# Attention backward for one query: dK of the previous pair ahead of the K blocks in the first turns

## The chip, the core and the metric

The kernel runs on one core of a Trainium2 chip. The core has TensorE (PE in the profile: matmuls, transposes, with PEld its weight loads), VectorE (DVE), ScalarE (ACT), GpSimdE (POOL) and SyncE (SP), each with its own instruction queue, worked in order; 16 DMA engines move data between the memory (HBM) and the on-chip memory (SBUF). TensorE writes to PSUM, the accumulator memory of eight banks. The metric is device time in microseconds (us) of one execution, lower is better.

## The reference

One query row per head attends to 8192 keys, for 32 heads of width 128, all in bfloat16; output and all three gradients are wanted.

```
scores = einsum('bhqd,bhkd->bhqk', q, k) * 128 ** -0.5     # 1 query, 8192 keys, 32 heads
attn   = softmax(scores)
out    = einsum('bhqk,bhkd->bhqd', attn, v)                # out_0
# vjp with grad_out (dO):
dP = dO . V^T        dS = attn * (dP - sum(attn * dP)) * 128 ** -0.5
dq = dS K  (out_1)   dK = dS^T q  (out_2)   dV = attn^T dO  (out_3)
```

K and V are 67.1 MB each and are read once; dK and dV are as large and are written once: 268.4 MB in all. dK and dV are outer products of a column of 8192 weights with a row of 128.

## The kernel before, in words

Heads go in pairs: pair j is heads 2j and 2j+1, 16 pairs, one turn of the main loop (L308) each, and a seventeenth turn that only finishes the last pair. K and V of a pair are one tile each, 128 partitions by 128 rows of 128 elements (4096 KB), `Kt[j]` and `Vt[j]`; three K tiles and two V tiles are held (`K_BUFS`, `V_BUFS`). dK and dV are written in place over `Kt[j]` and `Vt[j]` by VectorE and stored from there. All large transfers are issued from SP's queue in program order (`load_k`, `load_v`, `outer`). A load of K(j+2) needs the store of dK(j-1) to have landed (three buffers), a load of V(j+1) that of dV(j-1) (two buffers).

The steps of a pair, with the names that the change touches:

- K scores: `k_blocks` (L164) transposes an eighth of K in 32x32 blocks on VectorE into one of three `XK_sb` buffers; `k_scores` (L169) multiplies it by the query, four matmuls into `s_ps`. `blocks(n)` does both for the next n of the eight blocks, and only the second for a block that has been transposed already.
- Softmax: `s_back` turns the scores back (VectorE), maximum, `top`, a TensorE transpose into the shared bank `m_ps`, `nbias`, exponential (ScalarE), sum by a matmul, `rinv`, then `p_rep` and `window("p")` on ScalarE, and `p_s` on VectorE.
- V scores (dP): `v_transposes` (L186) turns four 128x128 squares of V on TensorE into one of three `T_ps` banks, `v_copy` (L196) copies the bank on ScalarE into `XV_sb`, and after eight such groups `v_scores` (L200) does 16 matmuls for half of the keys.
- `contract` (L234): 32 matmuls in 8 rounds of 4, of p with V (`acc_p`, which gives out) or dS with K (`acc_ds`, which gives dq). `gather_copy` copies the accumulator to SBUF, `gather` (L248) sums it by eight small matmuls into `m_ps` and copies two columns to `o_all` or `dq_all`.
- `v_back`, `pd_sum`, `ds_of`: dP is turned back, multiplied by the exponentials and summed, and dS is formed, its window on ScalarE.
- `outer` (L257): one eighth of dV or dK as one multiply on VectorE over the tile; it has to wait for the round of `contract` that reads this eighth. After the eighth one the store is issued. The last dK is stored in four quarters and the last dV in two halves (`PARTS`).
- `result` (L298): transposes `o_all` or `dq_all` and stores it from the one buffer `fin_sb`.

In each turn j the work of pair j (K scores, softmax, then V transposes, contraction with p and dV together, L409 to L418) is interleaved with what is left of pair j-1 (dP, dS, contraction with dS, dK). There are two forms, chosen by `ends` (L310). In the overlapped form (turns 2 to 15) the contraction with dS stands between the K blocks, and the eight multiplies of dK are spread: two before the softmax, two in its waits (L373, L389), four behind it. In the serial form (turns 0, 1 and 16) the contraction and the whole of dK stand after the second K block, the other K blocks follow (L342 to L357), and V transposes fill the waits of the softmax on TensorE. The order on each engine is as the program writes it (`manual_schedule`): there is no planner.

In the last turn the order is: `pd_sum`, `ds_of`, gather of out, its store, contraction with dS, eight multiplies of dK with four stores, and ahead of the fourth the gather of dq and its store (L346 to L348).

Of the kernel before, what the change touches and what calls it, by code (L numbers as in the profile page):

```python
# [14 lines left out]

XK_BUFS = 3
PARTS = {("dk", -1): 4, ("dv", -1): 2}
CH = 16
TB = 4
# [7 lines left out]
def kernel(  # L27
# [168 lines left out]
    def v_copy(j, c):  # L196
        b = c % (NX // TB)
        nc.scalar.copy(XV[j][:, b * TB:(b + 1) * TB, :], st[j].pop(("T", c))[:])  # L198
# [107 lines left out]

    DQ = NG // 4
    for j in range(HP + 1):  # L308
        p_ = j - 1
        ends = j in (0, 1, HP)  # L310
        x = st.setdefault(j, {})
        todo = list(range(NU)) if j < HP else []

        def blocks(n):
            for u in todo[:n]:
                if (j, u) not in XK:
                    k_blocks(j, u)
                k_scores(j, u)
            del todo[:n]

        if j == 0:
# [3 lines left out]
            q_window(0)  # L325
        blocks(1)
        if j > 0:
            v_back(p_)
            pd_sum(p_)
        blocks(1 if ends else 2)  # L330
        if j == 0:
            first = psT.tile([P, 512], F32, tag="T", name="first")
            rows_bc(0, first[:, 256:512])
            do_columns()
            do_window(0)
        if j > 0:
            ds_of(p_)
            gather(p_, "p", st[p_]["m"])
            if j == HP:
                result(o_all, out_0)  # L340
        if ends and j > 0:
            contract(p_, "ds", 0, NG)  # L342
            gather_copy("ds")
            for r in range(NU):
                outer(p_, "dk", r)
                if j == HP and r == NU - 3:  # L346
                    gather(p_, "ds", st[p_]["m"])
                    result(dq_all, out_1)  # L348
            if j + 1 < HP:
                load_v(j + 1)  # L350
        if j == HP:
            break
        for i in range(4):
# [14 lines left out]
        nc.tensor.transpose(x["m"][:, 128:256], top[:].to_broadcast([P, P]), ident_f[:])  # L368
        if ends:
            v_transposes(j, 0)  # L370
            v_transposes(j, 1)
        else:
            outer(p_, "dk", 2)  # L373
        nbias = small.tile([P, 1], F32, tag="nbias")
        for t in range(2):
# [6 lines left out]
                         skip_group_check=True)  # L382
        if ends:
            v_copy(j, 0)
            v_copy(j, 1)
            v_transposes(j, 2)
            v_transposes(j, 3)
        else:
            outer(p_, "dk", 3)  # L389
# [5 lines left out]
        x["p_s"] = small.tile([P, NT], F32, tag="p_s", name="p_s")  # L395
        nc.vector.tensor_scalar(x["p_s"][:], e[:], rinv[:], scale, op0=ALU.mult, op1=ALU.mult)
        if not ends:
            gather(p_, "ds", x["m"])
        if j + 1 < HP:
            rows_bc(j + 1, x["m"][:, 256:512])  # L400
            q_window(j + 1)
        if not ends:
            for r in range(4, NU):
                outer(p_, "dk", r)
            if j + 1 < HP:
                load_v(j + 1)
        elif j > 0:
            gather(p_, "ds", x["m"])
        for r in range(NU):  # L409
            for c in (2 * r, 2 * r + 1):  # L410
                if not (ends and c < 4):
                    v_transposes(j, c)
                if not (ends and c < 2):
                    v_copy(j, c)
            contract(j, "p", 4 * r, 4 * r + 4)
            if r % 4 == 3:
                v_scores(j, r // 4)
            outer(j, "dv", r)  # L418
# [3 lines left out]
        if 0 < j and j + 2 < HP:  # L422
            load_k(j + 2)

    order.__exit__(None, None, None)

# [29 lines left out]
```

## Time and profile before

| | |
|---|---|
| time, median of 3 runs | 645.21 us (642.86 to 646.59) |
| the profiled execution | 644.92 us, span 643.1 us |
| DVE busy | 518.9 us (81%) |
| PE busy | 501.6 us (78%), mean granted clock 0.832 |
| ACT busy | 223.2 us (35%) |
| SP's transfers | 268.46 MB in 97.8% of the 16 engines' span |
| HBM over the span | 417 GB/s |

The span runs from the first instruction to the last; the time has 1.8 us more around it. Busy time is of instructions, not of useful work: PE at a granted clock of 0.5 is busy for longer with the same matmuls. The slices of the page are 40 equal ones, 16.1 us each. A DMA issue is a short instruction on SP's queue (SPq), and what it moves comes later, behind all that was issued before. `Kt` and `Vt` are both loaded and stored: `Kt<-in_k_dram` is a load, `out_dram<-Kt` the store of dK.

### The profile page before, as it was taken

Reading aid. Unit: us, or ns where it says so; the run is one execution under the profiler, and the core shown is the slowest. Engines: PE = TensorE matmul, PEld = TensorE weight load, DVE = VectorE, ACT = ScalarE, POOL = GpSimd, SP = SyncE. Lnnn points to the kernel's source line nnn. Section 1 sums busy time; section 2 is a strip of 40 time slices with the busy share of each in tenths; the row PEclk is TensorE's granted clock in tenths of the full one; section 3 lists DMA queues with packets and bytes.
Section 4 is the critical chain, followed back from the end, with each engine's and each line's share of the span. In section 5 each row is a group of like instructions: output and inputs, shape, how many; then the busy total and the mean of one; then the engine's idle time right before and its main releaser. Section 6 shows DMA issues by size and latency. Waiting matters only on the chain.

```text
span 643.1 us, 8528 instructions
## 1 busy us (share of the span) xinstructions
PE 501.6 (78%) x3480; PEld 284.9 (44%) x3480; DVE 518.9 (81%) x654; ACT 223.2 (35%) x508; POOL 3.2 (0%) x10
## 2 busy tenths in 40 slices
PE   4885887878798787879777798787879778798780
PEld 1441534445363544536354363444526345363550
DVE  5678598887979888797887977889797887978873
ACT  2430524325151432515143160442515235151440
POOL 1000000000000000000000000000000000000000
PEclk9976897879978687997878886788897779878785
DMA  8999988999999999999999999999999999999996
GB/s 365 442 431 421 423 336 360 374 438 423 427 435 429 426 429 438 419 429 439 429 428 432 439 425 427 438 431 431 429 438 428 430 436 429 431 427 427 403 416 271
DMA packets 11318, 269.01 MB, mean 418 GB/s; under 512 B 1424, under 2 KB 1424, under 8 KB 1424
## 3 DMA queue, kind: packets, MB, share of 16 engines
q1 hardware_dynamic: 11184, 268.46, 97.8%
q8 instruction: 27, 0.44, 0.3%
q14 instruction: 11, 0.09, 0.0%
q10 hardware_dynamic: 96, 0.02, 0.0%
HBM read 134.23 MB, written 134.23 MB: 417 GB/s over the span
## 4 chain that ended last, share of the span: by engine, by line
PE 43%; DMA 32%; DVE 18%; ACT 4%; issue 2%; ACTq 0%; SPq 0%; DVEq 0%
DMA Kt<-in_k_dram 19%; PE s_ps L176 15%; PE T_ps L193 13%; DMA out_dram<-Kt 11%; DVE XK_sb L166 5%; DVE Kt L261 5%; PE m_ps L253 4%; PE acc_p L240 4%; PE acc_ds L240 4%; ACT XV_sb L198 2%; PE dp_ps L210 2%; DMA out_dram<-fin_sb 2%; DVE Vt L261 2%; DVE sT L183 1%; DVE dpT L221 1%
## 5 line engine op out<-in xcount | busy, mean ns | idle before, releaser
L261 DVE TENSOR_TENSOR Vt<-p_rep,qd 128x2048 bf16<-128x2048 bf16 x128 | 156.4, 1225 | 63.4 <-PE acc_p L240 52.7
L176 PE MATMUL s_ps<-XK_sb,q_win 128*128 128x512 bf16 x512 | 154.3, 437 | 46.4 <-DVE XK_sb L166 41.2
L193 PE MATMUL T_ps<-ident_f,Vt 128*128 128x128 f32 x1024 | 170.9, 321 | 0.0
L198 ACT COPY XV_sb<-T_ps 128x512 f32<-128x512 f32 x256 | 140.5, 588 | 87.2 <-PE T_ps L193 87.1
L166 DVE STREAM_TRANSPOSE XK_sb<-Kt 128x1024 f32<-128x1024 f32 x128 | 151.3, 1221 | 19.3 <-DMA Kt<-in_k_dram 11.1
L261 DVE TENSOR_TENSOR Kt<-ds_rep,qd 128x2048 bf16<-128x2048 bf16 x128 | 149.7, 1215 | 5.0 <-PE acc_ds L240 4.5
L193 PEld LDWEIGHTS T_ps<-ident_f,Vt 128*128 128x128 f32 x1024 | 136.3, 165 | 37.8 <-issue 22.1
L176 PEld LDWEIGHTS <-q_win 128*128 128x128 bf16 x512 | 51.6, 111 | 132.0 <-issue 102.5
L240 PE MATMUL acc_p<-Vt,win_p 128*32 128x512 bf16 x512 | 57.1, 439 | 0.8 <-ACT win_p L232 0.8
L210 PE MATMUL dp_ps<-XV_sb,do_win 128*32 128x512 bf16 x512 | 34.8, 385 | 12.4 <-ACT XV_sb L198 12.3
L240 PE MATMUL acc_ds<-Kt,win_ds 128*32 128x512 bf16 x512 | 41.6, 414 | 0.0
L246 ACT COPY S_ds<-acc_ds 128x512 f32<-128x512 f32 x16 | 9.4, 585 | 92.9 <-PE acc_ds L240 92.9
L232 ACT COPY win_ds<-ds 64x128 bf16<-64x128 bf16 x32 | 9.5, 296 | 79.3 <-DVE ds L291 79.1
L380 ACT ACTIVATE e<-sT,nbias 128x128 f32<-128x128 f32 x16 | 8.3, 516 | 69.9 <-DVE nbias L376 69.9
L253 PE MATMUL m_ps<-lane,S_ds 128*128 128x2 f32 x128 | 26.3, 327 | 6.1 <-DVE rinv L391 4.3
L253 PEld LDWEIGHTS m_ps<-lane,S_ds 128*128 128x128 f32 x128 | 24.9, 290 | 8.0 <-DVE rinv L391 5.5
L381 PE MATMUL m_ps<-rs,ones_f 128*128 128x1 f32 x32 | 8.2, 324 | 25.2 <-ACT e L380 25.2
L210 PEld LDWEIGHTS <-do_win 128*32 128x32 bf16 x512 | 14.3, 94 | 28.7 <-issue 21.9
L240 PEld LDWEIGHTS <-win_p 128*32 128x32 bf16 x512 | 13.2, 94 | 26.6 <-issue 26.3
L368 PE MATMUL m_ps<-ident_f,top 128*128 128x128 f32 x16 | 4.7, 296 | 23.7 <-DVE top L366 23.7
L183 DVE STREAM_TRANSPOSE sT<-s_ps 128x512 f32<-128x512 f32 x16 | 11.5, 717 | 14.2 <-PE s_ps L176 14.2
L240 PEld LDWEIGHTS <-win_ds 128*32 128x32 bf16 x512 | 9.6, 100 | 27.2 <-issue 27.2
(59 smaller groups left out, 207.0 us busy)
## 6 DMA issues: line engine op xcount, KB each, us to landing
Kt<-in_k_dram SPq DMA_DIRECT2D x15, 4096.0 KB, 29.2
out_dram<-Vt SPq DMA_DIRECT2D x15, 4096.0 KB, 28.0
out_dram<-Kt SPq DMA_DIRECT2D x15, 4096.0 KB, 22.3
Vt<-in_v_dram SPq DMA_DIRECT2D x14, 4096.0 KB, 28.9
Vt<-in_v_dram SPq DMA_DIRECT2D x8, 1024.0 KB, 19.7
Kt<-in_k_dram SPq DMA_DIRECT2D x4, 1024.0 KB, 8.1
out_dram<-Vt SPq DMA_DIRECT2D x2, 2048.0 KB, 15.1
out_dram<-Kt SPq DMA_DIRECT2D x4, 1024.0 KB, 9.7
```

Of the source, the lines that this page charges most:

```text
L166: nc.vector.transpose(XK[j, u][:].rearrange("p g w i -> p (g w i)"), slots(Kt[j], u, NU).rearrange("p g d -> p (g d)").bitcast(F32))
L176: nc.tensor.matmul(st[j]["s"][:], lhsT=q_win[:, c, at:at + P], rhs=cols[:, c // 2, c % 2], start=(u == 0 and c == 0), stop=(u == NU - 1 an ...
L183: nc.vector.transpose(sT[:].rearrange("p g r -> p (g r)"), x["s"][:])
L193: nc.tensor.transpose(T_ps[:, i, :], words[:, m * P:(m + 1) * P], ident_f[:])
L198: nc.scalar.copy(XV[j][:, b * TB:(b + 1) * TB, :], st[j].pop(("T", c))[:])
L210: nc.tensor.matmul(out[b * QD:(b + 1) * QD, :], lhsT=do_win[:, b // 2, e2, at:at + QD], rhs=cols[:, z, e2, :, b * QD:(b + 1) * QD], start= ...
L232: nc.scalar.copy(wins[which][t * M:(t + 1) * M, :, 4 * t:4 * t + 4], src[t * M:(t + 1) * M])
L240: nc.tensor.matmul(acc[which][b * QD:(b + 1) * QD, :], lhsT=wins[which][:, g, :], rhs=X[:, 4 * g:4 * g + 4, :].rearrange("p n d -> p (n d) ...
L246: nc.scalar.copy(S[:].rearrange("p j d -> p (j d)"), acc.pop(which)[:])
L253: nc.tensor.matmul(bank[:, at:at + 2], lhsT=S[:, i, :], rhs=pick[:, i, 0:2], start=(i == 0), stop=(i == 3), skip_group_check=True)
L261: nc.vector.tensor_tensor(slots(G, r, NU).rearrange("p n (a b) -> p n a b", b=R), slots(rep, r, NU).unsqueeze(2).to_broadcast([P, CH, D // ...
L380: nc.scalar.activation(e[:].rearrange("p (u g) -> p u g", u=NU), x["sn"], ACT.Exp, bias=nbias[:], scale=scale, accum_out=rs[:])
```

## The change

Turn 2 joins turns 0, 1 and 16 in the serial form (`EARLY = 3`). In turn 1 the second K block no longer stands ahead of dS; in turn 2 none does. In turns 1 and 2 the contraction with dS comes first, then the gather of out, then eight V transpose groups with their copies and the first half of the V scores (`half(j, 0)`), while VectorE does dK; all K blocks but the first of turn 1 come after dK. In the softmax of turn 1, where TensorE had transposed V, VectorE transposes the first three K blocks of pair 2 (`ahead`); in that of turn 2 nothing stands. In the loop over dV of turns 1 and 2 the contraction comes ahead of the transposes, eight groups are left, and the second half of the V scores and the gather of dq follow the contraction of r = 4. In turn 0 three groups of transposes instead of four stand in the softmax, and two of the copies stand behind p. In the last turn the gather of out, with its store, comes behind the contraction with dS, and the gather of dq and its store come after dK; the store of dq is the last transfer issued.

```diff
@@ -14,6 +14,7 @@
 PSUM = bass.MemoryType.PSUM
 
 XK_BUFS = 3
+EARLY = 3
 PARTS = {("dk", -1): 4, ("dv", -1): 2}
 CH = 16
 TB = 4
@@ -305,11 +306,24 @@
         nc.sync.dma_start(dst.rearrange("b h s d -> (b h s) d"), fin_sb[:])
 
     DQ = NG // 4
+    NC = NX // TB
+
+    def half(j, f):
+        for c in range(f * NC, (f + 1) * NC):
+            v_transposes(j, c)
+            v_copy(j, c)
+        v_scores(j, f)
+
     for j in range(HP + 1):
         p_ = j - 1
-        ends = j in (0, 1, HP)
+        early = 0 < j < EARLY
+        ends = j < EARLY or j == HP
         x = st.setdefault(j, {})
         todo = list(range(NU)) if j < HP else []
+
+        def ahead(u):
+            if j == 1:
+                k_blocks(2, u)
 
         def blocks(n):
             for u in todo[:n]:
@@ -323,32 +337,37 @@
             k_blocks(0, 1)
             q_columns()
             q_window(0)
-        blocks(1)
+        if j < 2 or not ends:
+            blocks(1)
         if j > 0:
             v_back(p_)
             pd_sum(p_)
-        blocks(1 if ends else 2)
+        if not ends:
+            blocks(2)
         if j == 0:
+            blocks(1)
             first = psT.tile([P, 512], F32, tag="T", name="first")
             rows_bc(0, first[:, 256:512])
             do_columns()
             do_window(0)
         if j > 0:
             ds_of(p_)
+        if ends and j > 0:
+            contract(p_, "ds", 0, NG)
+        if j > 0:
             gather(p_, "p", st[p_]["m"])
             if j == HP:
                 result(o_all, out_0)
         if ends and j > 0:
-            contract(p_, "ds", 0, NG)
             gather_copy("ds")
+            if early:
+                half(j, 0)
             for r in range(NU):
                 outer(p_, "dk", r)
-                if j == HP and r == NU - 3:
-                    gather(p_, "ds", st[p_]["m"])
-                    result(dq_all, out_1)
             if j + 1 < HP:
                 load_v(j + 1)
         if j == HP:
+            gather(p_, "ds", st[p_]["m"])
             break
         for i in range(4):
             blocks(1)
@@ -366,10 +385,11 @@
         nc.vector.tensor_scalar_mul(top[:], mx[:], scale)
         x["m"] = psM.tile([P, 512], F32, tag="m", name="m_ps")
         nc.tensor.transpose(x["m"][:, 128:256], top[:].to_broadcast([P, P]), ident_f[:])
-        if ends:
+        ahead(0)
+        if j == 0:
             v_transposes(j, 0)
             v_transposes(j, 1)
-        else:
+        if not ends:
             outer(p_, "dk", 2)
         nbias = small.tile([P, 1], F32, tag="nbias")
         for t in range(2):
@@ -380,12 +400,11 @@
         nc.scalar.activation(e[:].rearrange("p (u g) -> p u g", u=NU), x["sn"], ACT.Exp, bias=nbias[:], scale=scale, accum_out=rs[:])
         nc.tensor.matmul(x["m"][:, 0:1], lhsT=ones_f[:], rhs=rs[:], start=True, stop=True,
                          skip_group_check=True)
-        if ends:
+        ahead(1)
+        if j == 0:
             v_copy(j, 0)
-            v_copy(j, 1)
             v_transposes(j, 2)
-            v_transposes(j, 3)
-        else:
+        if not ends:
             outer(p_, "dk", 3)
         rinv = x["rinv"] = small.tile([P, 1], F32, tag="rinv", name="rinv")
         nc.vector.reciprocal(rinv[:], x["m"][:, 0:1])
@@ -394,8 +413,12 @@
         window("p", x["p"][:, :, 0].rearrange("p (g j) -> p g j", j=4))
         x["p_s"] = small.tile([P, NT], F32, tag="p_s", name="p_s")
         nc.vector.tensor_scalar(x["p_s"][:], e[:], rinv[:], scale, op0=ALU.mult, op1=ALU.mult)
+        ahead(2)
         if not ends:
             gather(p_, "ds", x["m"])
+        if j == 0:
+            v_copy(j, 1)
+            v_copy(j, 2)
         if j + 1 < HP:
             rows_bc(j + 1, x["m"][:, 256:512])
             q_window(j + 1)
@@ -404,17 +427,24 @@
                 outer(p_, "dk", r)
             if j + 1 < HP:
                 load_v(j + 1)
-        elif j > 0:
-            gather(p_, "ds", x["m"])
         for r in range(NU):
-            for c in (2 * r, 2 * r + 1):
-                if not (ends and c < 4):
-                    v_transposes(j, c)
-                if not (ends and c < 2):
-                    v_copy(j, c)
-            contract(j, "p", 4 * r, 4 * r + 4)
-            if r % 4 == 3:
-                v_scores(j, r // 4)
+            if early:
+                contract(j, "p", 4 * r, 4 * r + 4)
+                for c in (NC + 2 * r, NC + 2 * r + 1):
+                    if c < 2 * NC:
+                        v_transposes(j, c)
+                        v_copy(j, c)
+                if r == NU // 2:
+                    v_scores(j, 1)
+                    gather(p_, "ds", x["m"])
+            else:
+                for c in (2 * r, 2 * r + 1):
+                    if j > 0 or c > 2:
+                        v_transposes(j, c)
+                        v_copy(j, c)
+                contract(j, "p", 4 * r, 4 * r + 4)
+                if r % 4 == 3:
+                    v_scores(j, r // 4)
             outer(j, "dv", r)
         gather_copy("p")
         if j + 1 < HP:
@@ -422,6 +452,7 @@
         if 0 < j and j + 2 < HP:
             load_k(j + 2)
 
+    result(dq_all, out_1)
     order.__exit__(None, None, None)
 
 
```

## The prediction, made before the result was known

> **What bounds the kernel now.** I read the page's slices first, then the busy time in short stretches, then the DMA queue's issues in order of time, and last the engines' own timelines between 37 and 144 us. The page:
>
> ```profile
> span 643.1 us, 8528 instructions
> ...
> PEclk9976897879978687997878886788897779878785
> DMA  8999988999999999999999999999999999999996
> GB/s 365 442 431 421 423 336 360 374 438 423 427 435 429 426 429 438 419 429 439 429 428 432 439 425 427 438 431 431 429 438 428 430 436 429 431 427 427 403 416 271
> ```
>
> The DMA engines are full almost throughout at about 430 GB/s, so a transfer of 4096 KB (4.19 MB) takes 9.75 us of them. All K, V, dK and dV go through one queue in order. The three slices from 80 to 128 us (336, 360, 374) are the hole that the change is about. In steps of 2 us (the last two numbers are DMA share and GB/s, the one before them the granted TensorE clock):
>
> ```profile
> 80.00:82.00 2.00, 1.97 (x19) 1.12 (x18) 1.76 (x2) 1.72 (x4) 0.00 (x0) 1.00 0.28 115
> 82.00:84.00 2.00, 1.09 (x16) 0.44 (x16) 1.98 (x2) 1.22 (x4) 0.00 (x0) 1.00 0.00 0
> 104.00:106.00 2.00, 2.00 (x12) 1.23 (x10) 2.00 (x3) 1.34 (x3) 0.00 (x0) 0.50 0.04 16
> 106.00:108.00 2.00, 2.00 (x16) 1.62 (x12) 1.52 (x2) 0.72 (x3) 0.00 (x0) 0.50 0.62 262
> 138.00:140.00 2.00, 1.74 (x8) 1.65 (x8) 1.83 (x4) 1.07 (x3) 0.00 (x0) 0.50 1.18 508
> 144.00:146.00 2.00, 2.00 (x12) 1.43 (x11) 1.16 (x1) 0.83 (x2) 0.00 (x0) 0.50 1.21 524
> ```
>
> The queue runs dry twice, for about 3 us each, until a store is issued:
>
> ```profile
> 37.92 0.35 SPq L269 DMA_DIRECT2D out_dram<-Vt  x1
> 54.54 0.34 SPq L269 DMA_DIRECT2D out_dram<-Kt  x1
> 83.28 0.33 SPq L269 DMA_DIRECT2D out_dram<-Vt  x1
> 106.41 0.33 SPq L269 DMA_DIRECT2D out_dram<-Kt  x1
> 119.80 0.33 SPq L269 DMA_DIRECT2D out_dram<-Vt  x1
> 143.75 0.33 SPq L269 DMA_DIRECT2D out_dram<-Kt  x1
> 157.52 0.33 SPq L269 DMA_DIRECT2D out_dram<-Vt  x1
> ```
>
> These are dV0, dK0, dV1, dK1, dV2, dK2, dV3. Each dV takes the load of K behind it, each dK the load of V, so an issue brings 19.5 us of transfers. From the restart at 107.2 the queue holds dK1, V3, dV2, K4: 39.0 us, plus 1.4 us because 112 to 128 us ran at 392 GB/s instead of 430. It would be empty at 147.6, and dK2 comes at 143.75, in time by 3.9 less some 0.8 us from issue to first data (83.28 to about 84.1). From there nothing runs dry until the last turn. So what counts is when the queue gets past K4, and each issue up to dK2 must come in time. SP's order of issues is not changed; only their times are.
>
> **The change, turn 0.** One transpose group fewer ahead of the softmax, two copies behind p instead of before it: the first contraction comes some 0.5 us earlier, and the group left out (8 transposes 1.02 us, so 0.51) returns in the loop. Sum 0, between -0.6 and +0.6; dV0 stays at 37.9, and the queue has work until 80.
>
> **Turn 1.** The second K block leaves the path to dS: the sum of p*dp ends at 40.6 as now, pdt, ds and window (0.14, 0.48, 0.60) give 42.0 instead of 42.6, and the contraction no longer stands behind the gather of o (1.70 us) and starts at 42.05 instead of 44.68. dK follows 0.65 later and takes 9.17 for eight, as now: it ends at 51.9 (now 54.5). TensorE meanwhile does contraction (to 45.5), gather (1.05 to 1.7), eight transpose groups (0.51 each at full clock, 0.95 at half: 4.3 to 7.6), copy and dP matmuls (1.5): it is ready for K scores between 52.9 and 56. Seven blocks follow: VectorE 1.16 each from 51.9, TensorE 0.98 each; the scores end at 61.0 at best, 62.9 at worst; I take 61.6 (now 63.96). The softmax to p's window is now 5.13 (to 69.09). The K block of pair 2 before nbias fills a wait of 0.48 and adds 0.7, the one before rinv fills 1.11 and adds 0.06, and two copies (about 0.3) leave ScalarE: 5.6, so 67.2. The third fills VectorE's wait for the first contraction. In the loop contractions (0.33) stand ahead of two transpose groups (1.02) for four r, then dP (0.4 wait, 1.06) and the gather of dq (1.05) stand ahead of the contraction for r=5, and three dV of 1.235 follow: 0.4+5.4+1.06+0.4+1.05+0.33+3.7 = 12.3 at full clock. TensorE has idled over 5 us by then, and at half clock a round costs 2.45 (0.55+1.90) instead of 1.35: two such rounds add 2.2. 14.5, so dV1 goes at 81.7 (now 83.28), between 79.3 and 83.5. The loop of now, p's window to dV1, took 14.2.
>
> **Turn 2** turns from the overlapped form, where dK's multiplies fill the waits of the softmax (dV1 to dV2 36.5 us), into a serial one. From dV's end to win_ds 3.1 (the last turn shows 618.4 to 621.5, which also has no K block there); contraction 3.5, at half clock as in turn 1 since TensorE has waited over 5 us (3.49 there; 2.6 from eight rounds of 0.33); gather 1.5; transposes 6.4 (4.3 to 7.6, nearer the upper end since the gather's two-column matmuls stand before them); copy and dP 1.5; eight K scores 8.2, since only three blocks are ready and each of the other five needs one of three buffers back; softmax 5.1, with nothing of dK left to fill it; loop 14.5. Sum 43.8. The three blocks saved on VectorE (3.5 us) lie beside dK and are worth nothing, as TensorE is late there. dV2 goes at 125.5 (now 119.8), between 119 with everything at full clock and 130 with both stretches at half clock throughout. dK1 in exchange goes at 81.7+3.1+0.6+9.2 = 94.6 instead of 106.4, 8 us before the queue needs it.
>
> **The queue.** It restarts with dV1 at 82.5 (a hole of some 1 us instead of 3). dV1, K3, dK1, V3: 39.0, and 1.1 for the slow stretch after a restart (now dV1 and K3 took 84.1 to 104.7, 20.6): empty at 122.6. dV2 at 125.5 brings data at 126.3: a new hole of 3.7. dV2, K4 19.5+1.4: empty at 147.2. Turn 3 is the code of now, and dK2 comes 23.95 after dV2 (119.80 to 143.75): 149.45, data at 150.25, a hole of 3.0. Now K4 is through at 147.6 without a hole behind it. So 150.25-147.6 = 2.65 later, and a slow stretch of 1.4 follows the restart: **+4.05**. Later dV3 (163) and dK3 (186.2) come before the queue (169 and 190) is empty, and since turns take 37.5 of compute and 39.0 of transfers, nothing gives the loss back or adds to it.
>
> **The end.** Now out_0 goes out ahead of dK15:
>
> ```profile
> 622.70 0.34 SPq L305 DMA_DIRECT2D out_dram<-fin_sb  x1
> 625.26 4.87 SPq L269 DMA_DIRECT2D out_dram<-Kt  x3
> 632.91 0.33 SPq L305 DMA_DIRECT2D out_dram<-fin_sb  x1
> 633.35 0.37 SPq L269 DMA_DIRECT2D out_dram<-Kt  x1
> ```
>
> With the gather behind the contraction (3.25 at half clock) out_0 comes near 627.5, and dK15's first quarter, ready at 624.5, waits behind it in SP's queue until 627.9: up to +2.6 where the engines have no work, 0 where the second half of dV15 (issued 618.2, the DMA share is 0.98 from 620 to 630) still covers it. The last quarter is no longer behind out_1, which waited for out_0 to land: 632.0 instead of 633.35, up to -1.3. I take 0.
>
> The profiled execution took 644.92 (span 643.1 and 1.8 around it), 0.3 under the median of 645.21. 644.92+4.05 gives **649.0**.
>
> **A rule of the skill.** The rows show the clock at 0.50 after the softmax of turn 2 from 102.5 to 109.4 and of turn 3 from 136.7 to 146.9. The Trainium skill, "TensorE: Matmul & The Clock Gate", Part 1, has the clock halve after an idle window of about 3.4 us and return after one busy window; its section on HAM oscillation warns of longer gaps, which speaks against a turn in series. By that rule one window is lost per stretch and the sum would be that of rival 2; the trace has 6.9 and 10.2 us, so it is worse here.
>
> **Rivals.**
> 1. The queue never runs dry. If TensorE stays at full clock, turn 1 ends at 67.0+12.3 = 79.3 and turn 2 takes 3.1+2.6+1.05+4.3+1.5+7.9+5.1+12.3 = 37.9: dV2 at 117.2, dK2 at 141.9 with its data against 147.6, and at most one slow stretch: -5.7+1.4, 640.6. It decides from dV2 at 118.5 down. Against it: each softmax of turns 1 to 3 is followed by a stretch at 0.50. 0.08.
> 2. One half-clock window (3.4 us) per stretch, as at 71.8 to 75.2 of now: contraction and transposes 2 less, each loop about 0.7 less: dV2 at 122, dK2's data at 146.75: -0.85+1.4, 645.5. 0.30.
> 3. Half clock for 10 us in both loops and through all transposes: dV2 at 130, 653.5. 0.17.
> The forecast (dV2 between 123.5 and 128) has 0.45: 647 to 651.5.
>
> **How the numbers follow.** A measurement tells 0.5% (3.2 us) from no change. Faster is rival 1: 0.08. Within 0.5% (to 648.4): rival 2 less a little, and the lower part of the forecast: 0.34. Slower: the rest, 0.58. The range reaches from between rivals 1 and 2 to past rival 3: 643 to 655.
>
> **What would show it.** Right: dK1 issued near 95, dV2 near 125, dK2 near 149; the DMA near zero for some us before 126 and before 150, and almost full between 84 and 120; the slices of 80 to 112 us near 420 GB/s and those of 112 to 160 lower. In turn 2 VectorE waits for K scores with TensorE behind its transposes. Wrong: dV2 before 119 or no dry spell before dK2 (rival 1), or a dK15 delayed with idle DMA engines at 626.

## The result and the profile after

The changed kernel took 648.9 us in the median (644.36 to 651.08, 20 executions), the kernel before 643.81 us (642.1 to 646.59, 20 executions on the same chip): a ratio of 1.0063, with an interval of 1.0046 to 1.008. It is slower by 0.6%, a little more than the 0.5% that was taken as no change. The forecast of +4.05 us was 649.0 against 644.92; measured is +5.1 against the median of before. The profiled execution took 646.16 us and is one of the quicker of its kernel, so its single times understate the loss.

The page of the changed kernel:

```profile
span 644.4 us, 8519 instructions
...
PEclk9979777888869698886869778697967869987685
DMA  8999999988999999999999999999999999999996
GB/s 366 443 423 421 422 393 396 424 364 358 408 433 424 431 432 429 429 432 430 429 418 425 438 430 429 426 437 428 432 438 428 431 433 430 430 433 423 412 406 284
```

The dip that lay at 80 to 128 us (336, 360, 374 GB/s) has become shallower there (393, 396, 424), and a new one stands at 128 to 161 us (364, 358). The DMA queue's issues in order of time (start, duration) are dV0, dK0, dV1, dK1, dV2, dK2, dV3:

```profile
37.12 0.35 SPq L270 DMA_DIRECT2D out_dram<-Vt  x1
51.30 0.34 SPq L270 DMA_DIRECT2D out_dram<-Kt  x1
81.06 0.33 SPq L270 DMA_DIRECT2D out_dram<-Vt  x1
94.40 0.33 SPq L270 DMA_DIRECT2D out_dram<-Kt  x1
122.13 0.33 SPq L270 DMA_DIRECT2D out_dram<-Vt  x1
146.41 0.33 SPq L270 DMA_DIRECT2D out_dram<-Kt  x1
160.26 0.33 SPq L270 DMA_DIRECT2D out_dram<-Vt  x1
```

dV1 came 2.2 us earlier, dK1 12.0 earlier, dV2 2.3 later and dK2 2.7 later. In stretches of 2 us (busy time of PE, PEld, DVE, ACT and POOL, then granted clock, DMA share, GB/s):

```profile
82.00:84.00 2.00, 0.98 (x4) 0.93 (x4) 0.96 (x6) 0.13 (x1) 0.00 (x0) 0.50 0.85 360
...
142.00:144.00 2.00, 1.75 (x10) 1.56 (x10) 2.00 (x2) 1.03 (x4) 0.00 (x0) 0.50 0.53 229
144.00:146.00 2.00, 2.00 (x13) 1.65 (x12) 2.00 (x3) 1.24 (x4) 0.00 (x0) 0.50 0.00 0
146.00:148.00 2.00, 2.00 (x12) 1.57 (x8) 1.61 (x2) 0.99 (x2) 0.00 (x0) 0.50 0.62 262
```

Of the hole at 81 to 84 us a short dip is left (DMA share 0.85 at 82 to 84 us), and the one at 104 to 107 us is closed: dK1 (94.40) is in the queue 9 us before K3 lands (103.6). In exchange the queue is dry from about 143.7 us, when K4 has landed, to 147.2 us, when the first data of dK2 (issued 146.41) move. Before, dK2 was issued 4.8 us ahead of K4's landing.

**One number carries the whole time.** In all twelve profiled executions of this case, of both kernels and the ten that follow, the last landing comes 454.2 to 455.3 us after the load of K of pair 5 has landed (median of the 16 engines). So in these twelve profiles nothing that happens behind K5 moves the time by more than about a microsecond. This landing was at 187.3 us before and at 188.5 us in the profile of after. The experiments below are about what moves it.

### The profile page after: what moved, and what is told of

The parts are those of the page before. It is cut to its first block, busy times and chain, and to the rows that moved or that the text cites. A ratio compares the mean times of both kernels' runs of the same rounds, so it can differ in the third digit from the quotient of the medians.

```text
span 644.4 us, 8519 instructions
## 1 busy us (share of the span) xinstructions
PE 504.7 (78%) x3480; PEld 288.4 (45%) x3480; DVE 519.3 (81%) x654; ACT 223.1 (35%) x508; POOL 3.2 (0%) x10
## 4 chain that ended last, share of the span: by engine, by line
PE 47%; DMA 25%; DVE 18%; ACT 6%; issue 2%; DVEq 0%; ACTq 0%; SPq 0%
PE s_ps L177 15%; DMA Kt<-in_k_dram 15%; PE T_ps L194 14%; DMA out_dram<-Kt 11%; DVE XK_sb L167 6%; PE acc_ds L241 5%; DVE Kt L262 4%; PE m_ps L254 4%; PE acc_p L241 4%; ACT XV_sb L199 3%; DVE Vt L262 2%; PE dp_ps L211 2%; DVE sT L184 1%; ACT e L400 1%; PE m_ps L401 1%
## 5 line engine op out<-in xcount | busy, mean ns | idle before, releaser
L262 DVE TENSOR_TENSOR Vt<-p_rep,qd 128x2048 bf16<-128x2048 bf16 x128 | 156.3, 1225 | 64.0 <-PE acc_p L241 51.9
L177 PE MATMUL s_ps<-XK_sb,q_win 128*128 128x512 bf16 x512 | 152.0, 432 | 36.8 <-DVE XK_sb L167 32.0
L167 DVE STREAM_TRANSPOSE XK_sb<-Kt 128x1024 f32<-128x1024 f32 x128 | 151.4, 1222 | 19.0 <-PE s_ps L177 10.2
L194 PEld LDWEIGHTS T_ps<-ident_f,Vt 128*128 128x128 f32 x1024 | 138.3, 166 | 36.5 <-issue 21.8
L241 PE MATMUL acc_ds<-Kt,win_ds 128*32 128x512 bf16 x512 | 43.7, 438 | 4.6 <-ACT win_ds L233 4.6
```

The source lines that it names most:

```text
L167: nc.vector.transpose(XK[j, u][:].rearrange("p g w i -> p (g w i)"), slots(Kt[j], u, NU).rearrange("p g d -> p (g d)").bitcast(F32))
L177: nc.tensor.matmul(st[j]["s"][:], lhsT=q_win[:, c, at:at + P], rhs=cols[:, c // 2, c % 2], start=(u == 0 and c == 0), stop=(u == NU - 1 an ...
L194: nc.tensor.transpose(T_ps[:, i, :], words[:, m * P:(m + 1) * P], ident_f[:])
L241: nc.tensor.matmul(acc[which][b * QD:(b + 1) * QD, :], lhsT=wins[which][:, g, :], rhs=X[:, 4 * g:4 * g + 4, :].rearrange("p n d -> p (n d) ...
L262: nc.vector.tensor_tensor(slots(G, r, NU).rearrange("p n (a b) -> p n a b", b=R), slots(rep, r, NU).unsqueeze(2).to_broadcast([P, CH, D // ...
```

## The experiments

In the table are the issue times of three stores, the landing of K4 (what empties the queue ahead of dK2) and of K5, in us of each run's profiled execution, and the ratio of times to the kernel before, with its interval, from all executions. A landing is the median of those of the 16 engines. Each kernel was timed beside the kernel before on the same chip, but not all on one chip, so the ratios can be compared and the medians only roughly.

| kernel | dV1 | dV2 | dK2 | K4 landed | K5 landed | ratio |
|---|---|---|---|---|---|---|
| before | 83.3 | 119.8 | 143.7 | 148.5 | 187.3 | 1 |
| after | 81.1 | 122.1 | 146.4 | 143.7 | 188.5 | 1.0063 [1.0046, 1.008] |
| e1_tail_only | 82.0 | 119.0 | 142.8 | 147.1 | 185.9 | 1.0003 [0.9984, 1.0023] |
| e2_turn1_only | 83.2 | 119.0 | 142.9 | 147.4 | 186.2 | 1.0004 [0.9988, 1.0019] |
| e3_no_tail | 85.1 | 127.4 | 151.6 | 148.9 | 193.5 | 1.005 [1.0031, 1.007] |
| e4_warm | 83.4 | 120.2 | 144.3 | 144.7 | 186.4 | 0.9961 [0.9947, 0.9975] |
| e5_before_warm | 79.7 | 116.3 | 140.3 | 144.9 | 183.7 | 0.996 [0.9942, 0.9978] |
| e6_warm3 | 83.0 | 119.7 | 143.8 | 144.4 | 185.9 | 0.9962 [0.9942, 0.9982] |
| e7_late | 82.2 | 125.0 | 148.3 | 147.5 | 190.3 | 1.0036 [1.0021, 1.0052] |
| e8_no_ahead | 82.5 | 124.5 | 148.6 | 146.0 | 190.5 | 1.0045 [1.0028, 1.0062] |
| e9_both | 81.6 | 118.9 | 142.1 | 144.4 | 183.9 | 0.9994 [0.9977, 1.0011] |
| e10_both_turn0 | 79.4 | 116.8 | 139.9 | 142.3 | 181.6 | 0.9966 [0.9948, 0.9985] |

### The last turn alone

The kernel before with the last turn of the changed kernel: gather of out behind the contraction with dS, gather and store of dq at the end.

```diff
+            if j == HP:
+                contract(p_, "ds", 0, NG)
...
-            contract(p_, "ds", 0, NG)
+            if j < HP:
+                contract(p_, "ds", 0, NG)
...
-                if j == HP and r == NU - 3:
-                    gather(p_, "ds", st[p_]["m"])
-                    result(dq_all, out_1)
...
+            gather(p_, "ds", st[p_]["m"])
...
+    result(dq_all, out_1)
```

> The kernel before with only the last turn's new order. My theory (the loss is in turns 2 and 3, the end costs nothing): out_0 goes out some 4 us later than now, dK15's first quarter behind it, the DMA engines run low for about 2 us near 630, but the last of the 16 engines to finish, which trails the others by 4 us at the end of the kernel before, has work all the time: same time as before, within 0.7 us. Rival (the end matters): the four quarters follow the late out_0 one behind the other and the time is 1.5 to 3 us longer.

Measured: 645.66 us, ratio 1.0003. The issues of its last 20 us:

```profile
628.60 0.34 SPq L305 DMA_DIRECT2D out_dram<-fin_sb  x1
628.98 3.31 SPq L269 DMA_DIRECT2D out_dram<-Kt  x4
632.39 1.21 SPq L305 DMA_DIRECT2D out_dram<-fin_sb  x1
```

and the stretch in which the engines ran low:

```profile
628.00:630.00 2.00, 1.18 (x6) 0.99 (x6) 2.00 (x3) 0.73 (x2) 0.00 (x0) 0.50 0.30 119
```

The store of out went out at 628.60 us instead of 622.70, all four quarters of the last dK behind it, and the DMA share fell to 0.30. Still the end did not move. In the profile of before the last of the 16 engines finishes 4.4 us behind the median one, in that of e1 0.6 us behind: the hole looks like that of the engines which were ahead and would have waited at the end anyway. This reading compares two executions; the figure that does not depend on it is the time from K5's landing to the last one, 454.3 to 455.2 us in the five profiles with the new last turn and 454.2 to 455.3 in the seven with the old one. So the loss is not at the end.

### Turns 0 and 1 alone

The changed kernel with turn 2 back in the overlapped form, and the old last turn.

```diff
-EARLY = 3
+EARLY = 2
...
```

The lines left out put the old last turn back; they are those of the edit under "All but the last turn".

> The changed kernel with turn 2 in the overlapped form again and the last turn in the old order: what is left is the change of turns 0 and 1 with the three early K blocks. My theory (turn 2 in series makes dV2 and dK2 late): dV1 near 81, dK1 near 102 to 104, dV2 near 117, dK2 near 141; the first hole is smaller, the second stays at 1 to 3 us, none before dK2: 1 to 4 us faster than before, 640 to 643. Rival (the loss comes from turn 1's new order, the gather and dP matmuls inside the loop over dV): dV2 no earlier than 119.8 and the time no better than before.

Measured: 644.07 us, ratio 1.0004. Both theories missed: my gain of 1 to 4 us did not come, nor a loss. dV1 went at 83.2 us and dK1 at 105.3 (83.3 and 106.4 before), so both holes were still there. dK1 becomes early by the serial turn 2 alone, and the new order inside turn 1 moves dV1 by as much as one execution differs from another.

### All but the last turn

```diff
-        if ends and j > 0:
+        if early:
             contract(p_, "ds", 0, NG)
...
+                contract(p_, "ds", 0, NG)
...
+                if j == HP and r == NU - 3:
+                    gather(p_, "ds", st[p_]["m"])
+                    result(dq_all, out_1)
...
-            gather(p_, "ds", st[p_]["m"])
...
-    result(dq_all, out_1)
```

> The changed kernel with the last turn in the old order. My theory (turns 2 and 3 carry it): dV2 at 122 to 126, a hole before dK2, 646 to 650 as the changed kernel. Rival (the end carries it): 2 to 3 us faster than the changed kernel, 644 to 646.

Measured: 648.3 us, ratio 1.005. The loss is here: turns 0 and 1 alone cost nothing (e2), and with turn 2 in series it is back. dV0, dV2 and dK2 of this profile, and the stretches ahead of dK2:

```profile
41.27 0.35 SPq L270 DMA_DIRECT2D out_dram<-Vt  x1
...
127.42 0.33 SPq L270 DMA_DIRECT2D out_dram<-Vt  x1
151.56 0.33 SPq L270 DMA_DIRECT2D out_dram<-Kt  x1
```

```profile
148.00:150.00 2.00, 1.75 (x9) 1.56 (x10) 2.00 (x3) 0.87 (x4) 0.00 (x0) 0.50 0.00 0
150.00:152.00 2.00, 2.00 (x12) 1.23 (x11) 1.79 (x3) 1.17 (x2) 0.00 (x0) 0.50 0.00 0
```

Here nothing moves for 3.5 us (148.9 to 152.4) and K5 lands 6.2 us later than before. Turn 0, whose code is that of after, gave dV0 at 41.27 us instead of 37.12. Between 28 and 30 us the two rows of after and of e3 are, in this order:

```profile
28.00:30.00 2.00, 1.60 (x23) 0.85 (x24) 1.92 (x2) 1.07 (x2) 0.00 (x0) 1.00 1.22 524
```

```profile
28.00:30.00 2.00, 2.00 (x12) 1.23 (x11) 1.68 (x2) 0.91 (x3) 0.00 (x0) 0.50 1.18 508
```

At a granted clock of 0.50 TensorE did 12 instructions in place of 23. The two profiles are 4.9 us apart in time and 4.2 in dV0, so much of the changed kernel's spread (6.7 us) would come from turn 0; only profiled executions have a trace, so this is not shown for the others.

The half-clock stretch is not all of it. TensorE also reaches full clock later at the start in e3. The same 24 matmuls of turn 0's K scores, first in after and then in e3:

```profile
14.12 5.66 PE L177 MATMUL s_ps<-XK_sb,q_win 128*128 128x512 bf16 x24
```

```profile
14.38 7.29 PE L177 MATMUL s_ps<-XK_sb,q_win 128*128 128x512 bf16 x24
```

In e8 and e9, whose turn 0 is the same code and has no stretch at 0.50, these matmuls took 7.57 and 7.41 us, and dV0 went at 39.05 and 39.25 us. Nor is turn 0 the same in the two kernels: dV0 went at 37.3 to 38.6 us in the four profiles with the old order of turn 0 and at 37.1 to 41.3 us in the seven that have the new one and no idle matmuls in it, six of them later than any of the four. Whether the new order of turn 0 makes it late is not shown: no run changes turn 0 alone.

### The clock held up in turns 1 and 2

The changed kernel, with matmuls of the identity by itself into a free PSUM bank, which nobody reads, at the places where TensorE waits: 16 behind the loop over dV of turn 1, and in both turns 6 ahead of dS, 5 and 4 in the softmax, 5 ahead of the loop.

```diff
+    def warm(n):
+        if 0 < j < EARLY:
+            T_ps = psT.tile([P, 512], F32, tag="T", name="warm_ps")
+            for i in range(n):
+                nc.tensor.matmul(T_ps[:], lhsT=ident[:], rhs=ident[:].unsqueeze(1).to_broadcast([P, TB, P]),
+                                 start=True, stop=True, skip_group_check=True)
...
+            warm(6)
...
+        warm(5)
...
+        warm(4)
...
+        warm(5)
...
+        if j < EARLY - 1:
+            warm(16)
```

> The changed kernel with idle matmuls on TensorE, whose results nobody reads, in the waits of turns 1 and 2 (16 of 512 columns after the loop over dV of turn 1, 6 before the window of dS, 14 in each softmax), to keep the granted clock at 1. If the half clock makes turn 2 long: the clock stays at 1 from 50 to 120 us, contraction with dS 2.6 instead of 3.6, the loop over dV 12.3 instead of 14.1, dV1 near 79, dV2 at 117 to 118, dK2 at 141 to 142 before the queue is empty: 641 to 644. If the serial order itself is it and the clock is not: dV2 stays at 121 or later, 646 to 650.

Measured: 641.98 us, ratio 0.9961, against 1.0063 for the changed kernel: 1.0% less, from matmuls that compute nothing wanted. TensorE's timeline in turn 2 of after (start, us, operation), and then of e4:

```profile
84.53 3.60 PE L241 MATMUL acc_ds<-Kt,win_ds 128*32 128x512 bf16 x32 [1.47 <-ACT win_ds L233]
...
89.12 3.98 PE L194 MATMUL T_ps<-ident_f,Vt 128*128 128x128 f32 x32
94.90 7.91 PE L177 MATMUL s_ps<-XK_sb,q_win 128*128 128x512 bf16 x32
...
108.56 1.97 PE L194 MATMUL T_ps<-ident_f,Vt 128*128 128x128 f32 x8
```

```profile
80.23 3.63 PE L321 MATMUL warm_ps<-ident 128*128 128x512 bf16 x16
...
86.50 1.91 PE L241 MATMUL acc_ds<-Kt,win_ds 128*32 128x512 bf16 x32 [0.16 <-ACT win_ds L233]
...
89.26 3.98 PE L194 MATMUL T_ps<-ident_f,Vt 128*128 128x128 f32 x32
95.08 7.91 PE L177 MATMUL s_ps<-XK_sb,q_win 128*128 128x512 bf16 x32
108.34 1.10 PE L194 MATMUL T_ps<-ident_f,Vt 128*128 128x128 f32 x8
```

The contraction took 1.91 us instead of 3.60, eight transposes of the loop 1.10 instead of 1.97; what ran at full clock in both took the same. Turn 2, from dV1's issue to dV2's, took 36.7 us, against 41.1, 42.3 and 42.0 in after, e3 and e8, and 36.5 in the overlapped form of before. The granted clock of e4 is 1 from 72.6 to 120.3 us; in after it is 0.50 from 81.6 to 88.4 and from 105.5 to 112.3 us. dK2 went at 144.3 us, later than the 141 to 142 expected, since dV0 of this execution was at 40.9. So at full clock the serial form is as short as the overlapped one, which itself has a stretch at 0.50 (102.5 to 109.4 us of before): the 4 to 6 us that it costs here are those of the half clock.

### The kernel before with the same idle matmuls

My theory after e4 was that the gain needs both, the early dK1 and the full clock. The rival was that the clock alone does it. 24 idle matmuls stand during dK0, 10 in and behind the softmax of turn 1 and 9 in that of turn 2.

```diff
+    def warm(n):
+        if 0 < j < 3:
+            T_ps = psT.tile([P, 512], F32, tag="T", name="warm_ps")
...
+            warm(24)
...
+        warm(5)
...
+        if not ends:
+            warm(4)
...
+        if ends:
+            warm(5)
```

> The kernel before, its order unchanged, with the idle matmuls in turns 1 and 2 (24 while VectorE does dK0, 10 in the softmax of turn 1, 9 in that of turn 2). If the full clock alone made the gain of the changed order with idle matmuls: 641 to 643 here too. My theory (both are needed: the changed order issues dK1 at 95 and closes the second hole, the clock keeps dV2 and dK2 in time): dV1 near 81, dK1 near 104, so the holes stay at 1 to 3 us, dV2 near 117.5, dK2 near 141.5: 642 to 645, no more than 2 us under the kernel before.

Measured: 642.22 us, ratio 0.996, the same as e4. The two ranges of time overlap, and 642.22 lies in both; but the theory that the gain needs the changed order fell, since the old order has the same gain. The stores went 1.2 to 1.3 us earlier than the theory had them: dV1, dK1, dV2 and dK2:

```profile
79.67 0.33 SPq L269 DMA_DIRECT2D out_dram<-Vt  x1
102.82 0.33 SPq L269 DMA_DIRECT2D out_dram<-Kt  x1
116.34 0.33 SPq L269 DMA_DIRECT2D out_dram<-Vt  x1
140.33 0.33 SPq L269 DMA_DIRECT2D out_dram<-Kt  x1
```

and the two places where the kernel before ran dry:

```profile
80.00:82.00 2.00, 1.15 (x7) 0.57 (x6) 1.93 (x7) 0.27 (x2) 0.00 (x0) 1.00 0.92 393
...
100.00:102.00 2.00, 2.00 (x12) 1.58 (x12) 2.00 (x3) 1.30 (x4) 0.00 (x0) 0.50 0.27 115
```

dV1 came 3.6 us earlier than before and closed the first hole. The second stayed: K3 had landed at 101.3 us, and dK1 came at 102.82. e4 had closed the second (dK1 at 96.2) and kept the first (DMA share 0.04 at 82 to 84 us). So each of the two has one of the holes left, both are 0.4% under the kernel before, and e5 needed none of the reordering.

The idle matmuls worked in turn 1 alone. From dV0 to dV1 the clock is at 0.50 for 3.4 us in e5, against 20.5 in before, and the time from dV0 to dV1 is 41.2 us instead of 45.4. In turn 2 a stretch at 0.50 stands in e5 as in before (99.2 to 106.0 us), and dV1 to dV2 takes 36.7 us against 36.5.

### Idle matmuls in turn 3 too

27 more idle matmuls, in turn 3, on top of e4.

```diff
-        if 0 < j < EARLY:
+        if n and 0 < j <= EARLY:
...
-        warm(4)
+        warm(4 if early else 6)
...
-        if j < EARLY - 1:
+        if j < EARLY:
             warm(16)
```

> The changed kernel with idle matmuls as before and 27 more: 16 between turn 2 and turn 3 and 11 in the softmax of turn 3. My theory (the queue runs dry where a store comes late, and with idle matmuls in turns 1 and 2 dK2 at 144.3 was still just late): dK2 1 to 2 us earlier, no dry stretch before it: 640 to 642, up to 2 us under the version with idle matmuls in turns 1 and 2 alone. Rival (turn 3 is covered by the queue): no difference.

Measured: 641.25 us, ratio 0.9962, which can't be told from e4. dK2 went at 143.8 us, 24.1 after dV2 (24.2 in e4). The rival was right about the time; but the clock was not held up: between 120 and 148 us it is at 0.50 for 10.2 us, against 17.1 in e4. So the run shows that these 27 matmuls gave nothing, and not what turn 3 at full clock would give.

### Later stores of dV2 and dK2, and nothing else

The kernel before with 13 transposes on VectorE, into a tile that nobody reads, ahead of the first multiply of dV2.

```diff
+            if j == 2 and r == 0:
+                late = small.tile([P, 512], F32, tag="back", name="late")
+                for i in range(13):
+                    nc.vector.transpose(late[:], x["s"][:])
```

> The kernel before with 13 extra transposes of the scores on VectorE (0.72 us each, 9.3 us) behind dK1 and ahead of dV2, nothing else. dK1 stays near 106, dV2 comes near 125.5 instead of 119.8 and dK2 near 149.4 instead of 143.75. My theory (dK2 has 3.1 us to spare, each further us is lost, and a restart costs some 1.4 us more): a dry stretch before dK2 and 647 to 650. Rival (turns of 37.5 us of compute against 39 us of transfers win it back): 643.5 to 646.

Measured: 646.58 us, ratio 1.0036. The 9.7 us of work, what became of dV2 and dK2, and the stretch ahead of dK2's data:

```profile
106.21 9.71 DVE L421 STREAM_TRANSPOSE late<-s_ps 128x512 f32<-128x512 f32 x13
```

```profile
124.99 0.33 SPq L269 DMA_DIRECT2D out_dram<-Vt  x1
148.30 0.33 SPq L269 DMA_DIRECT2D out_dram<-Kt  x1
```

```profile
146.00:148.00 2.00, 2.00 (x12) 1.23 (x11) 2.00 (x3) 1.33 (x3) 0.00 (x0) 0.50 0.13 53
```

Half of the added work disappeared in waits that VectorE had anyway. dV2 slid by 5.2 us and dK2 by 4.6, the queue ran dry ahead of dK2 for 1.6 us, and the kernel lost 0.36%, within the interval of e3 (1.0031 to 1.007) and under that of the changed kernel (1.0046 to 1.008), whose dry spells here are longer: 3.5 us in after and in e3. The loss was a bit under the 647 to 650 expected. So stores that come late in this place are enough for a loss of this kind, with the order of before.

### Without the three K blocks of pair 2 in the softmax of turn 1

```diff
-            if j == 1:
+            if False:
```

> The changed kernel without the three early K blocks of pair 2. As I predicted them (worth nothing, since TensorE is late): softmax of turn 1 about 0.8 us shorter, turn 2 as long as in the changed kernel (41.1 from dV1 to dV2) or up to 0.5 longer: same time as the changed kernel. Rival (they shorten turn 2, whose scores then wait for VectorE at 1.16 a block from the end of dK on): turn 2 1.5 to 2.5 us longer, 1 to 2 us slower.

Measured: 647.13 us, ratio 1.0045, beside 1.005 and 1.0063 with the blocks. VectorE's eight blocks and TensorE's scores of turn 2:

```profile
95.71 9.12 DVE L167 STREAM_TRANSPOSE XK_sb<-Kt 128x1024 f32<-128x1024 f32 x8
```

```profile
97.00 8.91 PE L177 MATMUL s_ps<-XK_sb,q_win 128*128 128x512 bf16 x32 [0.34 <-DVE XK_sb L167]
```

The scores take 8.91 us instead of 7.91, by VectorE's rate instead of TensorE's, and turn 2 is as long as with the blocks (42.0 us against 41.1 and 42.3). They buy at most 1 us of the 3.5 us of VectorE's time that they move.

### Both forms together

The new turn 1, turn 2 overlapped with five instead of two multiplies of dK ahead of the softmax, the old last turn, and idle matmuls in turns 1 and 2 (e9); the same with eight idle matmuls in turn 0 (e10).

```diff
-EARLY = 3
+EARLY = 2
+LOW = 0
...
+        if n and LOW < j < 3:
...
-            outer(p_, "dk", 0)
-            outer(p_, "dk", 1)
+            for r in range(5 if j == 2 else 2):
+                outer(p_, "dk", r)
```

> Turn 1 in the new order, turn 2 overlapped, the last turn as before, idle matmuls in turns 1 and 2, and since turn 2 has three K blocks less to transpose, five dK multiplies stand ahead of its softmax instead of two. My theory (what counts is when K5 lands, and that no store finds the queue empty): dV1 near 80, dK1 near 99 ahead of the end of K3 at 101, dV2 near 116, dK2 near 140, no dry stretch after 84: K5 lands at 181 to 183, 639 to 641. Rival (with a full clock the start is bound otherwise, by loads): as the kernel before with idle matmuls, 642.

Measured: 643.09 us, ratio 0.9994. A miss: dK1 at 102.5 us came 0.7 us before K3 landed (103.2), where data take 0.8 to follow an issue, and dK2 at 142.1 came 2.3 us before K4 landed (144.4); K5 landed 3.4 us earlier than before in the profile (642.17 us), and over all executions there was no gain that can be told from none.

```diff
-LOW = 0
+LOW = -1
```

> The same with 8 idle matmuls in turn 0. dV0 left at 37.1 to 41.3 in executions of the same turn 0; if its clock makes that, dV0 stays near 37 to 38 and the times of the executions lie closer together, 638 to 641, 0 to 1.5 us under the version without; if not, no difference.

Measured: 641.65 us, ratio 0.9966. dV1, dK1, dV2 and dK2:

```profile
79.45 0.33 SPq L271 DMA_DIRECT2D out_dram<-Vt  x1
100.31 0.33 SPq L271 DMA_DIRECT2D out_dram<-Kt  x1
116.77 0.33 SPq L271 DMA_DIRECT2D out_dram<-Vt  x1
139.90 0.33 SPq L271 DMA_DIRECT2D out_dram<-Kt  x1
```

All four come before the queue is empty, dK1 only just (K3 landed at 101.1 us), and the profiled execution is the shortest profiled one of this study:

```profile
span 637.8 us, 8602 instructions
...
GB/s 366 439 428 410 431 426 403 408 429 431 423 426 426 426 431 437 428 434 428 433 436 433 431 428 428 428 439 436 426 431 431 427 435 435 436 427 417 396 418 268
```

But the executions range from 639.68 to 644.54 us, so the expectation that they would lie closer together missed, and the median is no better than that of e5, which leaves the order as it was. e4, e5, e6 and e10 are all 0.3 to 0.4% under the kernel before, and about 1% under the changed one.

## Why the prediction was right, point by point

**Turns 0 and 1.** dK0 was predicted at 51.9 us and went at 51.3, dV1 at 81.7 (measured 81.06), dK1 at 94.6 (94.40). In this profile the sums held to within 0.7 us. The step from dV0 to dV1, 43.8 us by the forecast (37.9 to 81.7), took 43.9, 43.8 and 43.4 us (after, e3, e8). What was mis-sized is turn 0: taken as 0 with bounds of 0.6 us, but dV0 went at 37.1, 41.3 and 39.0 us. From dV0 to dV1 the old order took 45.4, 44.7 and 43.7 us (before, e1, e7), so of the 1.6 us forecast for dV1 perhaps half is the change, and by e2 the time does not show it.

**Turn 2.** Predicted 43.8 us, measured 41.07 in this profile and 42.3 and 42.0 in e3 and e8. By its terms: dV's end to the window 3.5 (predicted 3.1), contraction 3.60 (3.5), gather 1.1 (1.5), transposes 4.0 (6.4), copy and dP 1.8 (1.5), K scores 7.9 (8.2), softmax 5.15 (5.1), loop 14.1 (14.5). The term that was mis-sized is the transposes: the clock was back at 1 when they began at 89.12 us, and the forecast had it at half for most of them. The half clock during the contraction and in the loop was right. Rival 2 had dV2 at 122, measured 122.13, but not for its reason of 3.4 us per stretch: both stretches at 0.50 are 6.8 us long (81.6 to 88.4 and 105.5 to 112.3 us). The first spared the transposes because it began while TensorE still waited for dS. The Trainium skill, "TensorE: Matmul & The Clock Gate", Part 1, has the full clock back after one busy window of about 3.4 us. These two stretches agree: in each TensorE is busy for part of the first 3.4 us (1.4 and 1.9 us) and all through the second. So the rule does not mean 3.4 us lost per stretch, as the prediction and its rival 2 read it. Not all stretches agree: in that from 40.6 to 50.8 us TensorE is busy all through the last two windows. Over the three profiles dV2 went at 122.1, 127.4 and 124.5 us (after, e3, e8): one with rival 2 and two in the forecast's 123.5 to 128, and most of the difference is that of dV0.

**The queue.** The hole of 3.7 us at dV2 is small or missing: V3 landed at 123.1 us in this profile, just after dV2's first data could move, and in e8 and e3, where V3 landed at 124.5 and 127.1 us and dV2 was issued at 124.50 and 127.42, the queue stood empty for about 1 us. The hole of 3.0 us ahead of dK2 is there: 143.7 us, when the median engine has landed K4, to 147.2, 3.5 us. The restart was taken at 1.4 us and costs about 2.4: from dK2's first data to K5's landing it took 41.1 to 41.3 us in the six profiles in which the queue had run dry there, and 38.7 to 38.9 us from K4's landing to K5's in before, e1, e2 and e5, where it had not. The kernel before has the same 41.3 us behind its own second hole, from dK1's first data at 107.2 us to K4's landing at 148.5, where the prediction counted 40.4 and set that landing at 147.6. So the restart was taken about 1 us too short on both sides of the subtraction, and that cancels.

With these figures the shift of K5 closes in each of the three profiles: dK2's first data moved at 147.2, 152.4 and 149.4 us (after, e3, e8) against K4's landing of 148.5 in before, which with the 2.4 us makes +1.1, +6.3 and +3.3 us; measured are +1.2, +6.2 and +3.2. That is the mechanism of the prediction, a dry spell ahead of dK2 and its restart.

**How much of the number is luck.** The sum of +4.05 us starts from dV0 at 37.9 us. The one profile of the changed kernel has dV0 at 37.1, and there the loss is only 1.2 us, because turn 2 was taken 2.7 us too long. The median of +5.1 us comes close to the forecast since, as far as the profiles show, dV0 mostly goes later than 37.9 us (six of the seven above). So two errors of opposite sign, turn 2 too long and turn 0 too early, stand behind a forecast that is off by one microsecond: the mechanism was right, and part of the agreement is luck.

**The end.** It was taken as 0 between -1.3 and +2.6; e1 measured 0 (1.0003). The stated reason, that dV15's second half covers the gap, is wrong: the DMA share does fall, to 0.37 at 628 to 630 us of the changed kernel,

```profile
628.00:630.00 2.00, 1.02 (x9) 0.80 (x8) 2.00 (x3) 0.82 (x4) 0.00 (x0) 1.00 0.37 156
630.00:632.00 2.00, 1.20 (x8) 1.12 (x8) 2.00 (x3) 0.67 (x3) 0.00 (x0) 0.78 0.55 221
```

and the prediction had named a dK15 delayed with idle DMA engines as a sign of being wrong. It came and cost nothing; what the traces of e1 and of before suggest in its place is the trailing engine, 4.4 us behind in the kernel before.

**The three K blocks.** Costed at nothing because TensorE is late there; by the ratios of e8 and e3 they are worth nothing that can be told from none. Without them VectorE sets the pace of the scores, for 1 us.

**The rivals.** Rival 1, TensorE at full clock and no dry spell ahead of dK2, is nearly what e4 built: 641.98 us where 640.6 was worked out, with turn 2 at 36.7 us (37.9 worked out), though dK2's data still came 0.4 us after K4 had landed. Its sum counts dK2's lead of 5.7 us over the queue as a gain, which it is not, since a store that comes before the queue is empty waits in it; e10, in which no store came after the queue was empty, had K4 landed at 142.3 us, 5.3 us ahead of the 147.6 of the prediction, so the figure comes out about right by chance. As a forecast for the changed kernel it failed for the reason given against it, the half clock after the waits.

**What stays open.** Why turn 0 of the same code gets full clock in one execution and half in another is answered in part by the traces. In all twelve profiles the granted clock changes only at whole steps of 3.41 us, and the steps lie differently against the program each time: the first rise to full clock comes at 12.8 to 13.3 us in four profiles and at 17.2 to 18.7 us in eight, though the K scores begin at 8.9 to 9.6 us in all. The Trainium skill, "TensorE: Matmul & The Clock Gate", Part 1, calls the window free-running, not reset when a kernel starts, and the traces agree. Which wait then costs a stretch, and whether the new order of turn 0 makes that more likely, is open. Why some 32 KB packets take longer behind a dry spell is open too, and so is why e9 gained nothing over all its executions, with dK2 in time and dK1 almost in its profile; turn 0, which e10 then held up, is the only difference from e10, and a single pair of runs does not settle it.

## What to carry to other kernels

Where one in-order queue carries everything, write down for each issue when the queue would run dry without it, and leave some us to spare (here 4 us were enough and 2.4 not quite); a reordering that makes one issue twelve us early and the next one three us late loses, because here only the late one counted. Price a serial stretch with the clock that its own waits will bring, not with the clock of the overlapped rows, and look at more than one profile of the stage ahead of it, whose spread moves all that follows. Before reordering, try a few idle matmuls in the waits: here they gave on the kernel before all that any reordering in this study gave.

## What the runs showed of the hardware that was not expected

- A store that comes when the queue is about to be empty costs more than the empty time. From K4's landing (or dK2's first data, if later) to K5's landing it took 38.7 to 38.9 us where dK2 was issued 4.2 to 4.7 us ahead of K4's landing (before, e1, e2, e5), 39.3 to 39.5 where it was 2.3 to 2.4 us ahead (e9, e10), and 41.1 to 41.3 where it was 0.6 us ahead or less, or behind (after, e3, e4, e6, e7, e8). In e6 the queue stood empty for only 0.2 us (144.4 to 144.6) and the 2.4 us are there in full. In the 13 us after dK2's first data 9 to 16% of the 32 KB packets, 1.21 us otherwise, took over 1.5 us in these six, up to 2.3; in before, e9 and e10 it was 1 to 2%.
- The 16 DMA engines drift apart: in the kernel before the last is 0.4 us behind the median shortly after a dry spell (dK1) and 4.4 us at the end. In the seven profiles with the old last turn it is 0.9 to 4.9 us behind at the end.
- The granted clock changes only at whole steps of 3.41 us, and these steps are not tied to the start of the program (first rise at 12.8 to 18.7 us).
- Half clock decided what this change costs: ratio 1.0063 without idle matmuls, 0.9961 with them. The kernel before with idle matmuls of its own is at 0.996, so then the two orders come out alike.
- The same code of turn 0 ended between 37.1 and 41.3 us, and with it the later stores moved.
